# Where the loads of v for the next batch stand in the order of the SP queue

## The chip, the cores and the metric

The kernel runs on one core of one Trainium2 chip, and the time is the device time of one execution in microseconds. Three runs of the kernel before gave 949.58, 953.18 and 954.36 us; the median is 953.18 us. The profile is that of one more execution, which took 956.7 us.

The engines have short names in the profile: PE is TensorE (matrix multiplications), with its weight loads as PEld; DVE is VectorE, ACT is ScalarE, POOL is GpSimd and SP is SyncE. SP computes nothing here: it issues DMAs. A queue name with a q behind it (SPq) is the instruction stream of that engine. Each engine takes its instructions in the order in which they are written, and an instruction that waits holds back all that stand behind it on the same engine.

## The reference

The kernel computes an attention without the S by S product, followed by a gated feed-forward layer over all tokens. With 8 batches, 8 heads, 576 rows and 64 columns a head:

```python
q_s = softmax of q over its 64 columns
k_s = exp(k - max of k over the 576 rows);  k_s = k_s / (sum over the rows + 1e-9)
kv  = einsum('bhsd,bhse->bhde', k_s, v)          # one 64 x 64 matrix a head
x   = einsum('bhsd,bhde->bhse', q_s, kv)         # 4608 tokens x 512
out = (sigmoid(x @ w_gate) * (x @ w_val)) @ w_out   # 512 -> 1536 -> 512
```

For the change it matters that the softmax of k goes over the rows: its maximum is one number for each of the 512 columns of a batch, and it must be known before the exponentials of k can be taken and multiplied by v.

## The kernel before, in words

The 4608 tokens are worked through in nine spans of 512. The first span is written out apart (it also converts the weights). From the second on, each span is six steps, and a step multiplies one sixth of the hidden layer:

- `g1` (matmuls at L696) makes the hidden values of the step by seven products of sums of weights and sums of activations. Four of the seven weight operands are sums that are kept in DRAM and loaded into the one buffer `s_sb`. As soon as PE has used one of the four, `more` has POOL issue the load of the same part for the next step (`s_load`, L288, 512 KB each). So each of these loads has about one step in which to land.
- DVE and ACT turn the result into hidden values (L714 to L737) and split these into two parts (L746, L747). PE writes the next step's products into the three PSUM tiles that these lines read and so set free.
- `g2` (L768) multiplies the hidden values of the step before by the output weights, which POOL loads too (`wo_load`, L238).

Beside the six steps of span w, the main loop prepares span w + 1, and starts on what span w + 2 needs. `side_a` and `side_b` do this, with n = w + 1 and the step's number p. Batch b = n is finished in them: in step 0 its k has the maxima subtracted (`k_sub`, L362) after the queries' maxima have been taken (`qn_max`, L459) and subtracted (L466); the rest of it in step 1, with the exponentials; in step 2 PE multiplies k by v (`k_mm`, L388); in step 4 PE multiplies the queries by the result (`x_mm`, L560).

`load_next(n, p)`, called at the end of `side_b`, does the same for one span further, batch b = n + 1:

- steps 1 and 3 load the transposed k (`kT_load`), steps 2 and 4 take its maxima on DVE (`k_max`, L316);
- step 4 then writes the maxima to DRAM (`k_max_send`, L329: 512 single numbers, 2 KB) and reads them back spread over all 128 partitions into `kmax_b` (`k_max_read`, L333). For b over 2 both are issued by SP, and the read-back waits for the send to land;
- step 5 loads the four query tiles of span n + 1 (`qn_load`, L445), the five tiles of k (`k_load`, L341) and the five tiles of v (`v_load`, L357).

The tiles of v have buffers of their own: two `v_` tiles and three parts of `f_last`. PE reads them in step 2 of the next span, and there is one set. What follows on SP after step 5 is, in the next span, the queries' maxima (`qn_send`, L451), the four stores of the span's output (L671), and the spread loads of those maxima (L491).

The order is written by hand (the schedule is manual): the order of the calls is the order on each engine. Semaphores are set by the framework.

Of the kernel before, what the change touches and what calls it, by code (L numbers as in the profile page):

```python
# [51 lines left out]
def attn_moe(ctx: ExitStack, tc: tile.TileContext, qf, qn, qT, k, kT, v, wg, wv, wo, out):  # L52
# [251 lines left out]
    def kT_load(b, hp, t=None):  # L304
        if t is None:
            t = kt_two[hp % 2]
            nc.sync.dma_start(out=t, in_=kT[b, hp * P:(hp + 1) * P])
        kT_sb[b, hp] = t

    def k_max(b, hp):  # L310
        if hp == 0:
            kmax[b], kneg[b], ksum[b] = (
                small.tile([P, NP], F32, name=f"k_{x}") for x in ("max", "neg", "sum")
            )
        m = kmax[b][:, hp:hp + 1]
        nc.vector.tensor_reduce(out=m, in_=kT_sb[b, hp], axis=AX.X, op=ALU.max)  # L316
        nc.vector.tensor_scalar(
            out=kneg[b][:, hp:hp + 1], in0=m, scalar1=-1.0, scalar2=None, op0=ALU.mult
        )

    def k_sum(b, hp):
        t = kT_sb.pop((b, hp))
        nc.scalar.activation(
            t, t, AF.Exp, bias=kneg[b][:, hp:hp + 1], accum_out=ksum[b][:, hp:hp + 1]
        )

    def k_max_send(b):
        kmax_row[b] = row = dpool.tile([DM], F32, name="kmax_row")
        (nc.sync if b > 2 else nc.gpsimd).dma_start(out=row.rearrange("(h p) -> p h", p=P), in_=kmax.pop(b))  # L329

    def k_max_read(b):
        kmb[b] = kmax_b
        (nc.sync if b > 2 else nc.gpsimd).dma_start(  # L333
            out=kmax_b, in_=kmax_row.pop(b).unsqueeze(0).broadcast_to([P, DM])
        )

    def k_load(b, t, kt=None):
        s0, n = KTILES[t]
        if kt is None:
            kt = ring.tile([P, DM], F32, name="ring")  # L340
        nc.sync.dma_start(out=kt[:n], in_=k[b, s0:s0 + n])  # L341
        kt_sb[b, t] = kt

    def v_load(b, t, vt=None):
        s0, n = KTILES[t]
        if vt is None:

            if t < 2:
                vt = v_two[t]
            else:  # L350
                vt = f_last[:, t - 2].rearrange("p n e -> p (n e)")
        v_sb[b, t] = vt
        src = v[b, s0:s0 + n]
        if b == 0:
            nc.sync.dma_start(out=vt[:n, :, 0:P], in_=src.rearrange("s (h e) -> s h e", e=P))
        else:
            nc.sync.dma_start(out=vt[:n], in_=src)  # L357
# [85 lines left out]
    def qn_load(w, c):  # L443
        t = ring.tile([P, T], F32, name="ring")
        nc.sync.dma_start(out=t, in_=qf[w, c] if w < NF else qn[w - NF, c])  # L445
        qn_sb[w, c] = t.rearrange("p (i d) -> p i d", d=D)
# [372 lines left out]
    def side_b(n, p):  # L819
        if p == 0:  # L820
            for hp in range(NP):
                q_spread(n, "m", hp)
        if p == 1:
            for hp in range(NP):
                qT_load(n, hp)
        if p == 2:
            for hp in range(NP):
                q_spread(n, "r", hp)
        if p == 3:
            for hp in range(NP):  # L830
                qT_mul(n, hp)
        if p == 4:
            for hp in range(NP):
                x_mm(n, hp)
                x_ev(n, hp)
            c_subs()
        load_next(n, p)

    def load_next(n, p, vs=range(5)):

        if n + 1 >= NW:
            return
        b = n + 1 if n + 1 < B else None
        if b is not None:
            if p == 1:
                kT_load(b, 0); kT_load(b, 1)
            if p == 2:
                k_max(b, 0); k_max(b, 1)
            if p == 3:
                k_sum(b, 0); k_sum(b, 1)  # L850
                kT_load(b, 2); kT_load(b, 3)
            if p == 4:
                k_max(b, 2); k_max(b, 3)
                k_max_send(b)
                if b > 2:
                    k_max_read(b)
        if p == 5:
            for c in range(NC):
                qn_load(n + 1, c)
            if b is not None:  # L860
                for t in range(5):
                    k_load(b, t)
                for t in vs:
                    v_load(b, t)

# [9 lines left out]
    def after_first(j):  # L877
# [32 lines left out]
        if j in (2, 5, 7, 9):  # L910
            load_next(1, {2: 1, 5: 2, 7: 3, 9: 4}[j])
        if j == 10:
            load_next(1, 5, range(2))
            for i in (B11, T1, T2, B21, T4):
                c_hi(i)
# [64 lines left out]
    for t in range(2, 5):  # L980
        n = KTILES[t][1]
# [212 lines left out]
```

## Time and profile before

| | |
|---|---|
| median of three runs | 953.18 us |
| profiled execution | 956.7 us, its span 954.7 us |
| PE busy | 934.0 us (98%) |
| DVE, ACT, POOL busy | 613.2, 487.5, 176.4 us |
| DMA | 257.94 MB, mean 270 GB/s |
| loads of v, 256 KB each, us to landing | 13.2 (`v`), 13.3 (`f_last`) |
| send of the maxima on SP, us to landing | 10.0 |

The span is the time from the first to the last instruction of the profiled execution. The profile tells what each instruction took, what an engine was idle for before it, and whose end released it. For a DMA it tells when it was issued and how long it took until it had landed. Idle time of an engine that PE never has to wait for costs nothing.

### The profile page before, as it was taken

The numbers are of one execution on the slowest core, as the hardware profiler recorded it, in microseconds if no ns is written. First come the engines' busy times: TensorE is split into PE (matmuls) and PEld (weight loads), VectorE is DVE, ScalarE is ACT, GpSimd is POOL, SyncE is SP. The second block draws the span as 40 slices with busy tenths as digits, with TensorE's granted clock in tenths as the row PEclk, the third lists the DMA queues.
The fourth block names the chain that finished last, engine by engine and source line by source line (L and its number), as shares of the span: only waits on it lengthen the run. The fifth ranks groups of instructions, "written<-read, shape, count | busy, mean of one in ns | idle before, by whom it ended". The sixth has DMA issues, their size and how long they took to land.

```text
span 954.7 us, 18008 instructions
## 1 busy us (share of the span) xinstructions
PE 934.0 (98%) x7218; PEld 855.6 (90%) x7218; DVE 613.2 (64%) x1014; ACT 487.5 (51%) x824; POOL 176.4 (18%) x334
## 2 busy tenths in 40 slices
PE   5999899999999999999999999999999999999998
PEld 4643544799999999999999999999999999999998
DVE  7698679876566566756684667477655755564242
ACT  4589787663456254626472646363635434533222
POOL 0110112321122111212111121121212121212220
PEclk8899999999999999999999999999999999999999
DMA  9977676999699979999799969996999779858672
GB/s 317 347 231 269 221 274 192 376 357 307 205 268 355 293 236 232 368 293 269 184 382 312 290 153 378 321 305 138 379 326 258 222 239 324 255 178 266 200 215 72
DMA packets 96610, 257.94 MB, mean 270 GB/s; under 512 B 15568, under 2 KB 18128, under 8 KB 96528
## 3 DMA queue, kind: packets, MB, share of 16 engines
q0 software_dynamic: 46304, 168.32, 58.7%
q1 hardware_dynamic: 50224, 88.48, 32.0%
q8 instruction: 57, 0.93, 0.4%
q14 instruction: 25, 0.20, 0.1%
HBM read 228.20 MB, written 28.56 MB: 269 GB/s over the span
## 4 chain that ended last, share of the span: by engine, by line
PE 85%; DVE 5%; DMA 5%; issue 2%; ACT 2%; POOL 0%; SPq 0%; POOLq 0%; DVEq 0%; ACTq 0%
PE gv L696 46%; PE acc L768 27%; PE gv L644 3%; PE at L388 3%; PE acc L678 2%; PE gv L560 2%; DMA s_sb<-s 1%; DMA kmax_row<-k_max 1%; DMA wo<-wo_hl 1%; PE at L560 1%; DVE s_sb L276 1%; DMA lent<-k_in 1%; DMA w_raw<-wg_in 1%; DVE s L250 1%; DVE a_w L276 1%
## 5 line engine op out<-in xcount | busy, mean ns | idle before, releaser
L696 PE MATMUL gv<-c_hl,s_sb 128*128 128x256 f32 x2304 | 277.7, 276 | 0.8 <-DMA s_sb<-s 0.8
L768 PE MATMUL acc<-wo_hl,h 128*128 128x256 f32 x2304 | 270.1, 277 | 0.0
L696 PEld LDWEIGHTS gv<-c_hl,s_sb 128*128 128x128 f32 x2304 | 269.1, 188 | 1.0 <-issue 1.0
L768 PEld LDWEIGHTS acc<-wo_hl,h 128*128 128x128 f32 x2304 | 265.3, 188 | 0.7
L696 PE MATMUL gv<-c_hl,a_w 128*128 128x256 f32 x1728 | 221.0, 277 | 0.4 <-DVE h L656 0.4
L696 PEld LDWEIGHTS gv<-c_hl,a_w 128*128 128x128 f32 x1728 | 207.4, 188 | 1.6 <-DVE h L656 0.6
L288 POOL DMA_DIRECT2D s_sb<-s x188 | 99.7, 530 | 304.3 <-PE gv L696 302.8
L722 DVE TENSOR_TENSOR sg<-gv,sg 128x512 f32<-128x512 f32 x48 | 33.1, 691 | 134.1 <-PE gv L696 134.0
L238 POOL DMA_DIRECT2D wo_hl<-wo x96 | 50.9, 530 | 296.2 <-PE acc L768 294.1
L714 ACT COPY sg<-gv 128x512 f32<-128x512 f32 x48 | 28.2, 588 | 143.2 <-PE gv L696 142.7
L724 ACT COPY sg<-gv 128x512 f32<-128x512 f32 x48 | 28.2, 587 | 104.5 <-PE gv L696 104.5
L644 PE MATMUL gv<-x,f_w 128*128 128x512 f32 x160 | 72.3, 605 | 2.9 <-DVE ring L527 2.9
L726 DVE TENSOR_TENSOR sg<-sg 128x512 f32<-128x512 f32 x48 | 33.2, 691 | 54.3 <-ACT sg L724 54.3
L644 PEld LDWEIGHTS gv<-x,f_w 128*128 128x128 f32 x160 | 30.5, 194 | 41.0 <-issue 35.1
L747 DVE TENSOR_TENSOR h<-sg,h 128x1024 fp32r<-128x1024 f32 x48 | 58.8, 1225 | 1.6
L735 DVE TENSOR_TENSOR sg<-sg 128x512 f32<-128x512 f32 x48 | 33.2, 693 | 33.6 <-ACT sg L729 33.6
L729 ACT ACTIVATE sg<-sg 128x512 f32<-128x512 f32 x48 | 30.4, 634 | 47.7 <-DVE sg L728 47.7
L719 ACT COPY sg<-gv 128x512 f32<-128x512 f32 x48 | 28.2, 587 | 37.4 <-PE gv L696 37.4
L716 ACT COPY sg<-gv 128x512 f32<-128x512 f32 x48 | 28.2, 587 | 36.2 <-PE gv L696 36.2
L678 PE MATMUL acc<-wo_t,h 128*128 128x512 f32 x96 | 43.4, 594 | 1.6 <-DVE h L656 1.6
L502 DVE TENSOR_TENSOR ring<-ring,q_b 128x512 f32<-128x512 f32 x28 | 18.7, 691 | 38.1 <-DMA ring<-qT_in 38.0
L678 PEld LDWEIGHTS acc<-wo_t,h 128*128 128x128 f32 x96 | 18.0, 190 | 24.7 <-issue 20.3
(154 smaller groups left out, 1066.6 us busy)
## 6 DMA issues: line engine op xcount, KB each, us to landing
s_sb<-s POOLq DMA_DIRECT2D x188, 512.0 KB, 7.9
wo_hl<-wo POOLq DMA_DIRECT2D x96, 512.0 KB, 6.3
s<-s_sb POOLq DMA_DIRECT2D x24, 512.0 KB, 5.5
out<-x SPq DMA_DIRECT2D x35, 256.0 KB, 9.2
ring<-k_in SPq DMA_DIRECT2D x28, 256.0 KB, 15.5
ring<-qn_in SPq DMA_DIRECT2D x28, 256.0 KB, 10.7
q_b<-q_m_row SPq DMA_DIRECT2D x56, 128.0 KB, 9.4
ring<-qT_in SPq DMA_DIRECT2D x28, 256.0 KB, 7.3
```

Of the source, the lines that this page charges most:

```text
L238: nc.gpsimd.dma_start(out=t.rearrange("p h e -> p (h e)"), in_=wo_dram[2 * p + i].bitcast(F32R))
L288: nc.gpsimd.dma_start(out=s_sb[:, i].rearrange("p h n e -> p (h n e)"), in_=s_dram[p][:, i * n:(i + 1) * n].bitcast(F32R),)
L388: nc.tensor.matmul(kvps[b][:, hp], lhsT=kt[:n, sl], rhs=vt[:n, sl], start=(t == 0 and hp == 0), stop=(t == len(KTILES) - 1 and hp == NP - ...
L644: nc.tensor.matmul(ps[n], lhsT=w[:, kt // 2, sl], rhs=x_0[:, kt], start=(kt == 0), stop=(kt == NK - 1),)
L678: nc.tensor.matmul(acc[0][m], lhsT=h_0[j][:, m * P:(m + 1) * P], rhs=wo_t[j // 2][:, j % 2], start=(j == 0), stop=(j == NJ - 1),)
L696: nc.tensor.matmul(ps[:, n], lhsT=lh(kt), rhs=c_hl[i][:, x, kt], start=(first and n == 0 and kt == 0 and lh is wh and x == 0), stop=(last ...
L722: nc.vector.tensor_tensor(out=sg[:, 0], in0=rr, in1=sg[:, 0], op=ALU.add)
L726: nc.vector.tensor_tensor(out=sg[:, 3], in0=sg[:, 3], in1=sg[:, 2], op=ALU.add)
L729: nc.scalar.activation(sg[:, 0:2, 0], sg[:, 0:2, 0], AF.Sigmoid)
L735: tt(out=sg[:, 0:2, 0], in0=sg[:, 0:2, 0], in1=sg[:, 0:2, 1], op=ALU.mult)
L747: nc.vector.tensor_tensor(out=lo, in0=sg[:, :, 0], in1=hi.bitcast(F32), op=ALU.subtract)
L768: nc.tensor.matmul(acc[w][m][:, es], lhsT=h[lh][:, i, sl], rhs=o[i][:, rh, es], start=(at == 0 and i == 0 and lh == 0 and rh == 0 and e == 0),
```

## The change

The five calls of `v_load` for batch b = n + 1 move from the end of step 5's list to step 4, for n over 1. In step 4 they stand between the call that sends the maxima and the call that reads them back: the send is issued, then the five loads of v, then the read-back. The query loads and the k loads stay in step 5, and with nothing behind them the next transfer that SP issues is the send of the queries' maxima. For n = 1 the loads stay where they were. The loads that move are those of batches 3 to 7, five spans with five loads each; the bytes and the buffers are the same.

```diff
@@ load_next
             if p == 4:
                 k_max(b, 2); k_max(b, 3)
                 k_max_send(b)
+                if n > 1:
+                    for t in vs:
+                        v_load(b, t)
                 if b > 2:
                     k_max_read(b)
         if p == 5:
@@
             if b is not None:
                 for t in range(5):
                     k_load(b, t)
-                for t in vs:
-                    v_load(b, t)
+                if n == 1:
+                    for t in vs:
+                        v_load(b, t)
```

## The prediction

> **What bounds the kernel now.** I read the page first, then the list of waits, then the instructions in order of time around the change. The rows of waits give engine, line, what was waited for, us in total, times, longest.
>
> ```profile
> span 954.7 us, 18008 instructions
> ...
> PE 934.0 (98%) x7218; PEld 855.6 (90%) x7218; DVE 613.2 (64%) x1014; ACT 487.5 (51%) x824; POOL 176.4 (18%) x334
> ...
> PE gv L696 <- DMA s_sb<-s: 0.8, 1, 0.8
> ...
> SPq L333 <- DMA kmax_row<-k_max: 47.9, 5, 10.1
> ...
> SPq L357 <- DMA ring<-qn_in: 24.2, 15, 2.5
> ```
>
> PE works 934.0 of 954.7 us, and the last wait of PE for data in the stretch that the change touches (the sends of batches 3 to 7, from 260 us on) is one of 0.8 us, for a load of weight sums `s_sb`. So what the change can win there is 0.8 us; everything else it does can only be hidden or lost. The span pays for a DMA only where an `s_sb` load comes too late for PE, or where a late load holds DVE so long that PE finds no free PSUM tile.
>
> SP's queue around the change, for batch 5 (start and length in us, operation, count):
>
> ```profile
> 458.83 0.38 SPq L329 DMA_DIRECT2D kmax_row<-k_max  x1
> 469.40 0.33 SPq L333 DMA_DIRECT2D kmax_b<-kmax_row  x1
> 469.82 2.65 SPq L445 DMA_DIRECT2D ring<-qn_in  x4
> 472.57 7.38 SPq L341 DMA_DIRECT2D ring<-k_in  x5
> 481.36 2.27 SPq L357 DMA_DIRECT2D v<-v_in  x2
> 485.24 3.92 SPq L357 DMA_DIRECT2D f_last<-v_in  x3
> ```
>
> and of the same stretch two loads on POOL's queue and two groups of matmuls that read loaded data:
>
> ```profile
> 461.18 0.53 POOL L288 DMA_DIRECT2D s_sb<-s  x1 [2.19 <-PE gv L696]
> ...
> 462.54 0.53 POOL L288 DMA_DIRECT2D s_sb<-s  x1 [0.83 <-PE gv L696]
> ...
> 474.21 2.88 PE L696 MATMUL gv<-c_hl,s_sb 128*128 128x256 f32 x24
> ...
> 508.21 1.95 PE L388 MATMUL at<-v,ring 128*128 128x128 f32 x16
> ```
>
> SP issues nothing from 459.2 to 469.4: the read-back of the maxima waits for their send to land. The v loads, issued 481.4 to 489.2, are wanted by PE at 508.2. What the DMA engines do meanwhile, in four windows: 463 to 472, 472 to 474, 474 to 484, 484 to 488 us. q0 holds POOL's loads, q1 those of SP; the columns are packets, MB, share of the 16 engines.
>
> ```profile
> DMA packets 228, 0.81 MB, mean 90 GB/s; under 512 B 30, under 2 KB 30, under 8 KB 228
> ...
> q0 software_dynamic: 214, 0.81, 67.7%
> ...
> q0 software_dynamic: 195, 0.68, 93.6%
> q1 hardware_dynamic: 50, 0.10, 15.2%
> ...
> q0 software_dynamic: 690, 2.53, 67.9%
> q1 hardware_dynamic: 760, 1.39, 42.0%
> ...
> q1 hardware_dynamic: 532, 0.95, 65.9%
> q0 software_dynamic: 179, 0.63, 42.3%
> ```
>
> Two things are to be seen. From 463 to 472 us only 0.81 MB goes through (90 GB/s, against 3.92 MB in 10 us, 392 GB/s, from 474 to 484), although two `s_sb` loads of 512 KB are pending; the send of the maxima is out in that time. This is not an idle bus that waits for work, it is a clogged one. And where both queues have work, packets go about one to one (690 and 760), which gives q0, with its larger packets, two thirds of the bytes: 0.253 MB per us against 0.139.
>
> **The change, part by part.**
>
> *Issues moved.* Five v loads (4 of 128 rows and one of 64, by 2 KB: 1.18 MB) go from the end of the last step's list to the gap after the send. SP has them out by about 461.5 (an issue takes 0.33 us, five and the gaps between them some 2.3), well inside its wait until 469.4, so the read-back's issue is not moved: 0 us. Their buffers were read last by the k times v product of the batch before, some 50 us earlier, so they don't wait. The `SPq L357 <- qn_in` row, three times a span, shows that a load also waits for one eight places earlier in SP's list; with the new order the third query load waits for v's first and so on, each time with seven transfers still in flight, so q1 doesn't run dry: 0. Were that cover gone, it is at most the 2.5 us of the row, inside DVE's room below.
>
> *The `s_sb` loads beside them.* The third and fourth `s_sb` load of that step (issued 461.18 and 462.54) must be there at 474.21 and 1.36 later (12 of the 24 matmuls), 13.03 us after issue both. The fourth's times to landing for batches 3 to 7, in order:
>
> ```profile
> s_sb<-s POOLq DMA_DIRECT2D x1, 512.0 KB, 11.4
> s_sb<-s POOLq DMA_DIRECT2D x1, 512.0 KB, 13.9
> s_sb<-s POOLq DMA_DIRECT2D x1, 512.0 KB, 11.5
> s_sb<-s POOLq DMA_DIRECT2D x1, 512.0 KB, 12.0
> s_sb<-s POOLq DMA_DIRECT2D x1, 512.0 KB, 10.8
> ```
>
> The room is 1.6, -0.9 (the 0.8 us wait), 1.5, 1.0 and 2.2 us. With v in q1 from 461.5 on, q0 loses a third of the 0.81 MB of the clogged window (0.27), and from 472 to 474 gets two thirds of 0.78 instead of 0.68 (0.16 less): 0.43 MB, which at 0.253 per us is 1.7 us. Bounds: 0 if v's packets use engine time that q0 can't, 3.5 us if q1 takes half of the bytes (0.41 + 0.28 MB at 0.197 per us). I take 1.7, since the measured split is two to one. Waits: 0.1 + 1.7 + 0.2 + 0.7 + 0 = 2.7 us.
>
> *What now comes behind v.* The read-back, the four query loads and the k loads follow 1.18 MB in q1. The read-back is wanted on DVE only behind the queries and stands ahead of them in q1, so it isn't what comes last. The queries are: DVE already waits for the fourth one.
>
> ```profile
> 485.25 0.69 DVE L459 TENSOR_REDUCE q_m<-ring 128x8 f32<-128x512 f32 x1 [1.25 <-DMA ring<-qn_in]
> ...
> 489.46 0.68 DVE L722 TENSOR_TENSOR sg<-gv,sg 128x512 f32<-128x512 f32 x1
> ...
> 498.69 1.52 PE L696 MATMUL gv<-c_hl,a_w 128*128 128x256 f32 x12
> ```
>
> Read-back and queries are 1.31 MB. Before: 0.10 by 474, then 0.139 per us, through at 482.7, and DVE has the last at 485.2, 2.5 later. After: 2.49 MB must go by; 0.27 by 472, 0.26 to 474, 1.39 to 484 leave 0.57, which at the 0.95 MB in 4 us of the next window is 486.4, and with the 2.5 us 488.9: 3.7 us later. If q0's missing 0.43 MB is made good just there, 1.8 more; at the flat 0.139 and with nothing moved before 472 it is (1.18 - 0.16) / 0.139 = 7.3. I take 4.4.
>
> Behind that wait on DVE stand the two subtractions of k and then L722, L726, L728, L735, L736, L737 of the hidden layer, which free the PSUM tiles that PE writes next. Where they had to catch up (batch 6) they went like this:
>
> ```profile
> 588.87 0.68 DVE L722 TENSOR_TENSOR sg<-gv,sg 128x512 f32<-128x512 f32 x1
> ...
> 592.39 0.42 DVE L737 TENSOR_TENSOR sg<-gv,sg 128x256 f32<-128x256 f32 x1
> ...
> 596.46 1.52 PE L696 MATMUL gv<-c_hl,a_w 128*128 128x256 f32 x12
> ```
>
> From L722 to the end of L737 they need 588.87 to 592.81, 3.94 us, and PE wants the tile at 596.46: room 3.65 us. By the same sum batch 5 has 498.69 - 3.94 - 489.46 = 5.3, which I take for batches 3, 4 and 7 too. A delay of 4.4 passes the room only in batch 6, by 0.75, of which 0.7 is already given by the wait for `s_sb` there: 0.1 us.
>
> *What leaves the crowded stretch.* 481 to 500 us no longer carries v. No PE wait lies there, so it wins nothing: 0, at best the 0.8 us of the one wait.
>
> Sum: 2.7 + 0.1 = **2.8 us** on the profiled execution's 956.7 us (span 954.7 and 2.0 around it), 959.5. That execution lies 3.5 above the median of the runs shown, so against the median: 953.18 + 2.8 = **956.0**.
>
> **The rivals.**
>
> *Half shares: the weight loads starve.* If in the clogged window v gets half of the bytes instead of a third, the fourth `s_sb` load is 3.5 us later and PE waits 1.9 + 3.5 + 2.0 + 2.5 + 1.3 = 11.2 us: 964.4. Against it stands the split of 690 to 760 packets; for it, that this split was measured in free flow, and no row shows q1 data beside q0 in the clog. The Trainium skill says on the page "DMA: Bandwidth & Descriptors", section "Queues, rings and completion order", that an engine goes round its queues packet by packet and that a packet holds several descriptors; were the 2 KB rows of v joined to packets as large as those of q0, half shares would follow. The packets of 1.39 MB / 760 = 1.8 KB here speak against it.
>
> *Nothing moves in the clog: the queries come late.* If v starts to flow only from 472, `s_sb` loses little (0.16 MB, 0.6 us, felt in batch 4 alone), but queries and k come 7.3 us later and DVE passes its room everywhere: 4 times 2.0 and 3.65 = 11.7 us: 964.9. It decides from a delay of about 5 us. For it: 90 GB/s in the clog with work pending. Against it: q1 speeds up to 0.24 MB per us from 484 on.
>
> *A small gain.* v flows through gaps that q0 can't use and the wait of batch 4 goes: 953.18 - 0.8 = 952.4. For it: engine shares of 68% in the clog. Against it: an engine that leaves pending loads at 90 GB/s has nothing to give.
>
> *The change does nothing*, because SP can't issue v early. The buffers and the gap of 10 us say that it can: 953.2.
>
> **How the numbers follow.** The likeliest case, 956.0, has 0.57, its own range 953 to 959; the starved weights 0.15, the late queries 0.15, gain or nothing together 0.13. The runs shown go from 949.58 to 954.36, so that within 0.5% (4.8 us) can't be told from no change. The likeliest case falls mostly within 4.8 us (0.50 of its 0.57); with gain and nothing (0.12 of 0.13) that is 0.62 for no change; slower takes 0.07 and the two rivals of 0.15 but 0.04 of them that stay under the bound, 0.33 in all; faster is 0.05 with the spread of the runs. The range runs from 951 (the small gain, less some of that spread) to 966 (both slow rivals).
>
> **What would show it.** After: SP's v rows right behind L329, the read-back still some 10 us behind its send; the fourth `s_sb` load of that step 1 to 2 us longer to land, and a few short PE waits for `s_sb`, the largest in batch 4; DVE's wait for the fourth query load grown from 1.2 to about 5 us; PE waits on DVE at most in batch 6. Waits of PE for `s_sb` in all five spans show half shares; waits of PE in the second product of the next span, with `s_sb` in time, show the late queries. The prediction is wrong if PE's pace between waits changes, if the send itself takes longer or shorter with v behind it, or if PE waits for something else than these two.

## The result and the profile after

The changed kernel takes 956.98 us in the median of its runs, the kernel before 952.62 us beside it: the ratio is 1.0058, with a 95% interval of 1.0041 to 1.0075. (The ratio is not the quotient of the two medians, which is 1.0046; the means of the twelve runs each lie 5.3 us apart.) A second series gave 1.0053 (1.0033 to 1.0073). It is slower by about 5 us. The profiled execution after took 956.8 us; its span is hardly longer than that of before (954.9 and 954.7 us) only because its first 170 us, which the change does not touch, happened to be 4 us shorter.

The page and PE's list of waits, after:

```profile
span 954.9 us, 18031 instructions
...
PE 933.6 (98%) x7218; PEld 854.4 (89%) x7218; DVE 614.0 (64%) x1014; ACT 487.7 (51%) x824; POOL 176.4 (18%) x334
...
PE gv L696 <- DMA s_sb<-s: 1.7, 4, 1.1
```

One wait of 0.8 us for a load of weight sums has become four that are listed, 1.7 us together. SP's queue for batch 5, after:

```profile
456.67 0.38 SPq L329 DMA_DIRECT2D kmax_row<-k_max  x1
457.14 0.94 SPq L357 DMA_DIRECT2D v<-v_in  x2
458.17 1.56 SPq L357 DMA_DIRECT2D f_last<-v_in  x3
465.73 0.33 SPq L333 DMA_DIRECT2D kmax_b<-kmax_row  x1
466.15 3.79 SPq L445 DMA_DIRECT2D ring<-qn_in  x4
```

The five loads of v go out right behind the send, and the read-back stands 9.1 us behind the send, where it stood 10.6 before. Over the five spans the mean distance did not change: 10.0 us before, 10.1 after. The fourth `s_sb` load of that step, for batches 3 to 7:

```profile
s_sb<-s POOLq DMA_DIRECT2D x1, 512.0 KB, 14.3
s_sb<-s POOLq DMA_DIRECT2D x1, 512.0 KB, 13.2
s_sb<-s POOLq DMA_DIRECT2D x1, 512.0 KB, 13.2
s_sb<-s POOLq DMA_DIRECT2D x1, 512.0 KB, 13.7
s_sb<-s POOLq DMA_DIRECT2D x1, 512.0 KB, 13.4
```

All five are over the 13.03 us that PE leaves them; before, one was. The mean went from 11.9 to 13.6 us. What PE makes of it, in order of time behind the send of batch 3 (start, length, line, operation, count):

```profile
272.44 1.52 PE L696 MATMUL gv<-c_hl,s_sb 128*128 128x256 f32 x12
275.08 1.68 PE L696 MATMUL gv<-c_hl,s_sb 128*128 128x256 f32 x12 [1.12 <-DMA s_sb<-s]
276.59 1.58 PE L696 MATMUL gv<-c_hl,a_w 128*128 128x256 f32 x12
278.01 5.82 PE L768 MATMUL acc<-wo_hl,h 128*128 128x256 f32 x48
...
307.69 1.58 PE L696 MATMUL gv<-c_hl,a_w 128*128 128x256 f32 x12
309.10 1.95 PE L388 MATMUL at<-v,ring 128*128 128x128 f32 x16
...
319.41 1.52 PE L696 MATMUL gv<-c_hl,a_w 128*128 128x256 f32 x12
```

The wait is not the whole price. Behind it twelve matmuls take 1.58 us instead of 1.52, and the 48 of L768 take 5.82 instead of 5.60. This goes on until the next matmuls of another shape (L388), and then the pace is as before.

Because PE has hardly any other gaps in the main loop, the start of each L768 group can be laid beside that of another kernel; the difference then shows in which step time was lost. Here is the loss of the main loop in us against the kernel with two of the five loads moved (below), which has no wait there, worked out from these starts:

```text
                    batch 3   then slow   batch 4   then slow   5     6     7     loop in all
before                 0        0.6         1.2        1.2      0     0     0        3.0
after                  1.5      1.2         0.6        1.2      0.5   0.8   0.6      6.5
after, again           0.3      0           1.1        1.2      0.7   0.7   0.4      4.3
```

(Row "after, again" is another execution of the changed kernel. 0.3 us of the row "after" was lost ahead of the first of the sends. Columns 3 to 7 are the product behind each send, "then slow" is the slower pace in the steps that follow.) The execution of before that was profiled was not a typical one: it lost 3.0 us to one wait and to slow pace, and took 956.7 us. The 12 runs of the same kernel beside the result lie between 948.0 and 955.8, and the 29 of each of the two series below between 947.5 and 954.5.

Now the clog itself. The first fence is 464 to 470 us before, the second the same 6 us behind the send after (462 to 468; the send stands 2.2 us earlier there). Columns: packets, MB, share of the 16 engines.

```profile
q0 software_dynamic: 70, 0.25, 67.0%
```

```profile
q1 hardware_dynamic: 354, 0.64, 74.1%
q0 software_dynamic: 48, 0.19, 21.7%
```

v moves 0.64 MB in a stretch in which the weights alone got 0.25 MB through. So the clog holds the weight loads, but not v to the same degree.

### The profile page after: what moved, and what is told of

Same layout as the page of the kernel before. It is cut to its first block, busy times and chain, and to the rows that moved or that the text cites. A ratio compares the mean times of both kernels' runs of the same rounds, so it can differ in the third digit from the quotient of the medians.

```text
span 954.9 us, 18031 instructions
## 1 busy us (share of the span) xinstructions
PE 933.6 (98%) x7218; PEld 854.4 (89%) x7218; DVE 614.0 (64%) x1014; ACT 487.7 (51%) x824; POOL 176.4 (18%) x334
## 4 chain that ended last, share of the span: by engine, by line
PE 77%; DMA 11%; issue 4%; DVE 4%; ACT 2%; POOL 1%; SPq 1%; POOLq 0%; DVEq 0%; ACTq 0%
PE gv L696 42%; PE acc L768 24%; DMA s_sb<-s 6%; PE gv L644 3%; PE at L388 3%; PE acc L678 2%; DMA x<-wg_in 1%; PE gv L560 1%; DMA kmax_row<-k_max 1%; DMA wo<-wo_hl 1%; DMA ring<-k_in 1%; PE at L560 1%; DVE s_sb L276 1%; DMA wo_raw<-wo_in 1%; SPq L355 1%
## 5 line engine op out<-in xcount | busy, mean ns | idle before, releaser
L768 PE MATMUL acc<-wo_hl,h 128*128 128x256 f32 x2304 | 270.4, 277 | 0.0
L768 PEld LDWEIGHTS acc<-wo_hl,h 128*128 128x128 f32 x2304 | 265.5, 188 | 0.7
L722 DVE TENSOR_TENSOR sg<-gv,sg 128x512 f32<-128x512 f32 x48 | 33.2, 691 | 153.0 <-PE gv L696 153.0
L714 ACT COPY sg<-gv 128x512 f32<-128x512 f32 x48 | 28.2, 588 | 143.9 <-PE gv L696 110.1
L729 ACT ACTIVATE sg<-sg 128x512 f32<-128x512 f32 x48 | 30.4, 634 | 48.3 <-DVE sg L728 48.3
L728 DVE TENSOR_TENSOR sg<-gv,sg 128x512 f32<-128x512 f32 x48 | 33.2, 692 | 4.7 <-PE gv L696 2.2
## 6 DMA issues: line engine op xcount, KB each, us to landing
ring<-qn_in SPq DMA_DIRECT2D x28, 256.0 KB, 11.2
```

Source lines behind the costliest of these rows:

```text
L722: nc.vector.tensor_tensor(out=sg[:, 0], in0=rr, in1=sg[:, 0], op=ALU.add)
L728: nc.vector.tensor_tensor(out=sg[:, 1], in0=z, in1=sg[:, 1], op=ALU.add)
L729: nc.scalar.activation(sg[:, 0:2, 0], sg[:, 0:2, 0], AF.Sigmoid)
L768: nc.tensor.matmul(acc[w][m][:, es], lhsT=h[lh][:, i, sl], rhs=o[i][:, rh, es], start=(at == 0 and i == 0 and lh == 0 and rh == 0 and e == 0),
```

## The experiments

Each was timed beside the kernel before, in two series. In the series of the first three kernels below and of the packed send with v late, the kernel before has a median of 950.28 us; in the series of the other four it has 949.93 us. Each of these kernels was profiled in one execution, the changed one in two.

**v behind the read-back.** The loads stay in step 4, but SP reaches them only when the send has landed:

```diff
                 k_max_send(b)
-                if n > 1:
-                    for t in vs:
-                        v_load(b, t)
                 if b > 2:
                     k_max_read(b)
+                if n > 1:
+                    for t in vs:
+                        v_load(b, t)
```

> The five v loads stay in step 4 but stand behind the read-back of the maxima, so SP issues them only when the send has landed. Weights theory (the loss comes from s_sb loads that share the engines with v while the send is out): the fourth s_sb load of the step lands within 0.6 us of before (11 to 12.6 us, batch 4 about 14), PE waits as before, ratio to the kernel before 0.999 to 1.002. Queries theory (v ahead of queries and k holds DVE up): queries land about 7 us later than before, PE waits about 2 us a span behind DVE, ratio 1.008 to 1.013.

987.51 us, ratio 1.0403 (1.0379 to 1.0427). The weight loads were indeed on time (fourth load 10.1 to 12.3 us). The queries theory had the cause right, late queries, but the engine and the price wrong: it expected PE behind DVE, about 2 us a span, and PE waits almost only for a copy on ACT, 26.8 us in all. The waits of PE, then DVE and ACT in the step behind the send of batch 3:

```profile
PE gv L696 <- ACT sg L714: 26.8, 5, 6.0
```

```profile
286.43 0.69 DVE L459 TENSOR_REDUCE q_m<-ring 128x8 f32<-128x512 f32 x1 [5.08 <-DMA ring<-qn_in]
...
295.84 0.68 DVE L722 TENSOR_TENSOR sg<-gv,sg 128x512 f32<-128x512 f32 x1
```

```profile
297.76 0.63 ACT L729 ACTIVATE sg<-sg 128x512 f32<-128x512 f32 x1 [5.67 <-DVE sg L728]
...
300.28 2.19 ACT L470 ACTIVATE ring<-ring 128x512 f32<-128x512 f32 x4
302.38 2.69 ACT L367 ACTIVATE ring<-ring 128x512 f32<-128x512 f32 x5
304.98 0.56 ACT L714 COPY sg<-gv 128x512 f32<-128x512 f32 x1
```

The chain goes on from DVE to ACT: behind the late sigmoid (L729) ACT still has the exponentials of queries and k (L470, L367), and only then the copy L714, which PE waits for. The kernel before has the same order, without a gap:

```profile
495.34 2.20 ACT L470 ACTIVATE ring<-ring 128x512 f32<-128x512 f32 x4
497.44 2.70 ACT L367 ACTIVATE ring<-ring 128x512 f32<-128x512 f32 x5
500.25 0.59 ACT L714 COPY sg<-gv 128x512 f32<-128x512 f32 x1
```

The copy ends at 500.84, and PE's next product into that tile starts at 498.69 + 24 matmuls (2.72) = 501.41. The room on ACT is 0.6 us. And a wait of this length costs more than itself. Two windows of the same kernel (the last three columns are granted clock, DMA share, GB/s), the wait and what follows:

```profile
301.00:305.50 4.50, 0.05 (x1) 0.00 (x0) 4.50 (x8) 4.50 (x10) 0.53 (x1) 0.78 1.13 310
305.50:310.00 4.50, 4.41 (x20) 4.41 (x21) 0.98 (x3) 1.10 (x3) 0.53 (x1) 0.50 1.17 240
```

After 4.5 us without a matmul PE runs at half clock (0.50) for 4.5 us; behind the other four waits, of 4.7 to 6.0 us, it does so for some 3 to 6 us. The Trainium skill ("TensorE: Matmul & The Clock Gate", Part 1) has the clock halve after an idle window of about 3.4 us and come back after as long a time of work; the trace agrees for waits of 4.5 to 6.0 us. The 4% slower pace behind the short waits above is something else: the granted clock shows 1.00 there.

**v ahead of the send.** The same five lines stand ahead of `k_max_send(b)`. Nothing holds SP there, so the loads go out with the end of step 3, 20 us ahead of the send.

> The five v loads stand in step 4 ahead of the call that sends the maxima; SP is free then from about 20 us earlier, so they go out at the end of step 3. Weights theory: v is through before the send, the fourth s_sb load lands as before (10.8 to 13.9 us), ratio 0.998 to 1.001. Queries theory: queries have v out of their way, ratio 0.998 to 1.001 too, with DVE's wait for the fourth query load gone. If early bytes cost wherever they stand: ratio 1.004 to 1.007.

950.19 us, ratio 0.9995 (0.9980 to 1.0010); no wait of PE for `s_sb` is listed, fourth load 10.3 to 13.0 us. Early loads as such cost nothing. They win nothing either: DVE's wait for the fourth query load became shorter (0.6 us for batch 5, between 0 and 1.1 in the others) without going altogether, and it was hidden before.

**Two of five, four of five.** Only the first two, or four, of the loads move:

```diff
                 if n > 1:
-                    for t in vs:
+                    for t in range(2):      # or range(4)
                         v_load(b, t)
...
-                if n == 1:
-                    for t in vs:
-                        v_load(b, t)
+                for t in (vs if n == 1 else range(2, 5)):      # or range(4, 5)
+                    v_load(b, t)
```

> As changed, but only the first two of the five v loads move (0.52 of 1.18 MB); three stay at the end of step 5. Weights theory, delay in proportion to the bytes: the fourth s_sb load is 0.7 us later than before instead of 1.6 (mean of five about 12.6 us), one or two short waits of PE, ratio 1.000 to 1.003. Threshold instead of proportion: the same as with five, ratio 1.004 to 1.007, landing 13.2 us or more.

> As changed, but the first four of the five v loads move (1.05 of 1.18 MB), the last stays at the end of step 5. Two of five cost nothing. If there is a free gap in the stretch of the send which the fifth load or the third to fifth overfill: four of five lies between, the fourth s_sb load lands at 12.3 to 13.3 us, ratio 1.001 to 1.004. If only the fifth load is at fault: ratio 1.000, landing 11 to 12 us.

Two: 950.64 us, ratio 1.0005 (0.9989 to 1.0022). Four: 950.36 us, 1.0003 (0.9987 to 1.0020). The fourth weight load for batches 3 to 7, first with two, then with four moved:

```profile
s_sb<-s POOLq DMA_DIRECT2D x1, 512.0 KB, 10.2
s_sb<-s POOLq DMA_DIRECT2D x1, 512.0 KB, 12.7
s_sb<-s POOLq DMA_DIRECT2D x1, 512.0 KB, 10.8
s_sb<-s POOLq DMA_DIRECT2D x1, 512.0 KB, 11.5
s_sb<-s POOLq DMA_DIRECT2D x1, 512.0 KB, 11.2
```

```profile
s_sb<-s POOLq DMA_DIRECT2D x1, 512.0 KB, 12.6
s_sb<-s POOLq DMA_DIRECT2D x1, 512.0 KB, 12.5
s_sb<-s POOLq DMA_DIRECT2D x1, 512.0 KB, 12.4
s_sb<-s POOLq DMA_DIRECT2D x1, 512.0 KB, 12.3
s_sb<-s POOLq DMA_DIRECT2D x1, 512.0 KB, 13.4
```

The means are 11.3 us with 0.52 MB ahead, 12.6 with 1.05 MB, 13.6 with 1.18 MB. With no v in that stretch they are 11.9 (before), 11.2 (v ahead) and 10.7 us (v behind the read-back), so the first 0.52 MB cost nothing that stands out from this scatter, which speaks against a delay in proportion; neither of the two landings forecast for two loads, 12.6 and 13.2 us or more, came. Then the delay eats the room, and with the fifth load it is gone. With four, the landing is the one forecast for a free gap that is overfilled (12.3 to 13.3 us), but the time is not (1.001 to 1.004): only batch 7's load is over 13.03, and PE has one wait of 0.3 us for it. In the next step of that span PE also waits for the copy L714 on ACT, behind a tile of k that reached DVE late (a line of DVE, then one of PE):

```profile
683.07 0.69 DVE L362 TENSOR_TENSOR ring<-ring,kmax_b 128x512 f32<-128x512 f32 x1 [1.37 <-DMA ring<-k_in]
693.44 1.65 PE L696 MATMUL gv<-c_hl,s_sb 128*128 128x256 f32 x12 [0.41 <-ACT sg L714]
```

This is the narrow room on ACT once more: DVE takes up L722 34.0 us behind the send there, against 30.7 in batch 7 before.

**The clog taken away.** The send writes the maxima in the order in which they lie in a partition, 128 pieces of 16 bytes instead of 512 of 4, and the subtraction reads the spread row in that order:

```diff
-        ...dma_start(out=row.rearrange("(h p) -> p h", p=P), in_=kmax.pop(b))
+        ...dma_start(out=row.rearrange("(p h) -> p h", p=P), in_=kmax.pop(b))
...
-        eng.tensor_tensor(out=kt[:n], in0=kt[:n], in1=kmb[b][:n], op=ALU.subtract)
+        o = kt[:n].rearrange("p (h q) -> p h q", q=P)
+        m = kmb[b][:n].rearrange("p (q h) -> p h q", h=NP)
+        eng.tensor_tensor(out=o, in0=o, in1=m, op=ALU.subtract)
```

(Batch 0, whose maxima are not sent, keeps the old line.) It was run with v late as before, with v as changed, and with v ahead of the send.

> The kernel before, with v at the end of step 5, but the maxima are sent as 128 pieces of 16 bytes instead of 512 of 4 (the order of the row in DRAM changes, and the subtraction from k reads it in that order). If the small writes make the clog: the four s_sb loads of the step land in 8 to 10 us, PE's wait for s_sb goes, ratio 0.996 to 1.000. If something else makes it: landing 11 to 14 us as before, ratio 0.999 to 1.001.

> The changed kernel with the maxima sent as 128 pieces of 16 bytes. Weights theory (v harms only together with the clog of the small writes): the fourth s_sb load lands in 5 to 9 us, no wait of PE for s_sb, ratio to the kernel before 0.997 to 1.000 as with v late (0.9985). If v costs s_sb its time without the clog too: landing over 12 us in some span, ratio 1.001 to 1.005.

> The packed send, with the v loads ahead of the send's call. Neither theory sees a wait left for v to add: no PE wait for s_sb, ratio 0.997 to 1.000; if the wait for the queries on DVE had cost anything in the kernel before, it would be lower still, 0.995 to 0.997.

v late: 949.22 us, ratio 0.9985 (0.9973 to 0.9997). v as changed: 949.57 us, 0.9992 (0.9979 to 1.0004). v ahead: 949.39 us, 0.9997 (0.9985 to 1.0009). In none of the three does PE wait for `s_sb`. The fourth load with v late, batches 3 to 7:

```profile
s_sb<-s POOLq DMA_DIRECT2D x1, 512.0 KB, 5.0
s_sb<-s POOLq DMA_DIRECT2D x1, 512.0 KB, 5.5
s_sb<-s POOLq DMA_DIRECT2D x1, 512.0 KB, 8.0
s_sb<-s POOLq DMA_DIRECT2D x1, 512.0 KB, 6.6
s_sb<-s POOLq DMA_DIRECT2D x1, 512.0 KB, 5.5
```

and SP's send and read-back for batch 5 of the same kernel:

```profile
449.72 0.33 SPq L329 DMA_DIRECT2D kmax_row<-k_max  x1
454.13 0.33 SPq L333 DMA_DIRECT2D kmax_b<-kmax_row  x1
```

The read-back follows the send after 4.4 us instead of 10.6, and the weights land in half the time (8 to 10 us were expected): the send of 512 small pieces is the clog. With v as changed the fourth load takes 8.4 to 9.5 us (5 to 9 were expected), so v still costs the weights some 3 us, but out of a room of 13: without the clog the change is harmless. With v late this send is faster than the kernel before, by a little more than the measurement is uncertain; the three kernels with it cannot be told apart.

**The changed kernel again.**

> The changed kernel once more, unaltered, for a second profile and times beside the next three. Weights theory: again all five of the fourth s_sb loads land in 13.0 us or more and PE loses 0.4 to 1.6 us in each of the five spans; ratio 1.004 to 1.007. If the loss was chance of one stretch: waits in other places, ratio nearer 1.000.

955.17 us, ratio 1.0053. All five fourth loads landed in 13.2 to 13.9 us; the losses are the third row of the table. Behind the sends they recur in the same five places, each time with other sizes; the slow pace recurs only behind batch 4.

## Why the prediction was right or wrong

The predicted 956.0 us lies close to the measured 956.98, and the range holds it. The highest chance, 0.62, went to no change within 0.5%: the two ratios, 0.58 and 0.53%, are just past that, and both intervals reach below it, so this stays undecided. The closeness of the number is in part luck. The forecast difference was 2.8 us and the measured one is about 5, and two errors of the sum cancel, as is told below under DVE's room.

*Issues moved:* right. v's rows stand behind the send, and the read-back keeps its distance.

*The `s_sb` loads beside them:* the place and the mean delay were right (1.7 us forecast, 1.6 measured), the way to it was wrong. The step took it that v would take a third of the 0.81 MB that went through the clog anyway. It took three quarters of the bytes of a traffic that more than tripled (0.64 and 0.19 MB where there had been 0.25). What q0 lost lies mostly at the two ends of the clog. In the fences that follow, the first rows are the 3 us in which the send's 512 writes go out, before (461 to 464) and after (459 to 462); the last is 470 to 472 after, when the bus frees itself (0.68 MB in the same 2 us before):

```profile
q0 software_dynamic: 133, 0.48, 109.1%
q1 hardware_dynamic: 528, 0.00, 11.3%
```

```profile
q1 hardware_dynamic: 728, 0.38, 82.9%
q0 software_dynamic: 75, 0.24, 23.9%
...
q0 software_dynamic: 138, 0.50, 74.9%
```

With the 2 us between these stretches, in which q0 moved a little more after (0.51 MB, 468 to 470) than before (0.45 MB, 470 to 472), q0 lost 0.42 MB in the 13 us. The forecast was 0.43: the delay came out right because these bytes did, and that v could take so much more than its third without costing q0 more was not foreseen. The sum "0.1 + 1.7 + 0.2 + 0.7 + 0" laid one delay over the rooms of one execution. In both profiled executions after, all five loads came late, and the products behind the sends lost 3.9 and 3.2 us.

*What was left out:* the pace behind a wait. The prediction names a change of PE's pace between waits as a sign that it is wrong, and the pace did change. It cost 2.3 and 1.2 us in the two executions after, and the step priced a wait at its own length. This is most of the way from 2.8 to the measured 5 us; the rest is probably that the sum started from an execution which had already one such wait and its slow pace in it, while the medians of before (950.28 and 949.93 us) lie close to that of a kernel whose profiled execution has none (950.64 us with two loads moved). That the median run of before has no such wait is inferred from the times; only the one execution was profiled.

*What now comes behind v:* wrong. Queries were to come 4.4 us later. DVE took up the fourth query tile of batch 5 26.4 us behind the send before (485.25 - 458.83), and 26.0 us after:

```profile
482.70 0.69 DVE L459 TENSOR_REDUCE q_m<-ring 128x8 f32<-128x512 f32 x1 [0.75 <-DMA ring<-qn_in]
```

v was mostly through by then, because it could use the clogged stretch: 1.02 of 1.18 MB had moved on q1 by 468 us, and the queries were issued from 466.15. Where it can't, behind the read-back, the queries come about 6 us late, as the rival without movement in the clog had it.

*DVE's room:* wrong, for that rival and for the prediction's own sum. 5.3 us were worked out from DVE alone. ACT, with its exponentials ahead of the copy L714, has 0.6 us, and behind the waits of 4.5 to 6.0 us the clock halves. So the rival's 11.7 us were 37 us when an experiment made it happen. In batch 3 there the fourth query tile was taken up about 6.2 us later behind the send than before, and PE waited 4.5 us: seen from the queries the room was 1.7 us. Had they come 4.4 us late in the changed kernel, as forecast, each span would have lost about 2.7 us by that room (an estimate from batch 3) and not 0.1 in all. The term came out near nothing because the delay, too, was wrong.

*What leaves the crowded stretch:* right, nothing is won there. v ahead of the send gives 0.9995.

*The rivals:* the sign given for half shares did appear, as the fourth `s_sb` load was late and PE lost time behind the send in all five spans, and v took even more than half of the bytes in the clog; but the price did not, 3.9 and 3.2 us in place of 11.2, because most of v's bytes came on top of those of q0. The small gain did not occur, nor did the late queries in the changed kernel. The wait of batch 4 did not go: the product behind its send lost 0.6 and 1.1 us. The largest loss was to be there; it was in batch 3 in one execution and in batch 4 in the other.

## What to carry to other kernels

A queue that waits is not a bus that is free: look at the bytes per us in the stretch into which a load is to move, and ask why pending work doesn't move there. Where a load must land within a step, its room is the number to watch: here 1.05 MB beside it cost no time that could be measured, and 1.18 MB about 5 us. And the room behind a late operand ends at the engine that stands last in the chain, with all that is queued ahead of the instruction that frees the buffer, not at the first engine that waits.

## What the hardware showed that was not expected

- 512 writes of 4 bytes held the weight loads up for some 6 us after nearly all of them had gone out (528 packets of q1 from 461 to 464, then 0.25 MB in 6 us, against 392 GB/s later); with 128 writes of 16 bytes, the same 2 KB, the read-back follows the send after 4.4 us in place of 10.6. The Trainium skill ("DMA: Bandwidth & Descriptors", Specifications) has writes under 512 bytes read, change and write back; both sends are under that bound, so the bound alone does not explain the difference. The number, the length and the places of the writes changed together; which of them decides was not tried.
- In the clog q1's loads moved 0.64 MB while q0's pending weights moved 0.19. Why the two queues fare so differently was not tried.
- Behind some short waits of PE the same matmuls take 4% longer at a granted clock of 1.00, for 34 to 37 us, until matmuls of another shape come: after waits of 0.8, 1.1, 0.2 and 0.5 us, but not after others of 0.2 to 0.4 us, and once, before, for 13 us (338 to 351) without a listed wait. The DMA share was as high in the same steps of a kernel at the usual pace (1.17 from 380 to 415 us with two of five loads moved, 1.14 after). The cause stays open.
